# Score products of the first 16 items over 128 contraction rows, 60 of them zero, instead of 68

## The chip, the cores and the metric

One core of one Trainium2 chip runs the whole program in one launch. The metric is device time in microseconds of that core. An execution that is profiled has a span (first to last instruction) and an own time, which is a little longer.

## The reference

Attention with a decaying bias, then a gated two-layer feed-forward, then a soft mixture of experts. The attention is what the change touches:

```python
scores = scale * np.matmul(q, k.transpose(0, 1, 3, 2))        # scale = 1/8, 64 dimensions
cum = np.cumsum(np.maximum(s, 0.0), axis=-1)
bias = -(cum[:, :, :, None] - cum[:, :, None, :])
scores = np.where(causal, -1000000000.0, scores + np.minimum(bias, 0.0))
attn = softmax(scores)
x = attn @ v                       # 4 batches, 8 heads, 576 tokens, 64 dimensions
h = (x @ w1) * (x @ w2) @ w3       # the feed-forward: "gl" products in the kernel
...                                # then 32 slots, 8 experts, and the way back
```

## The kernel before

The attention is cut into items. An item is one head with some of its five query tiles; `ITEMS` lists the first eight heads with tiles 0 to 2 as items 0 to 7, the same heads with tiles 3 and 4 as items 8 to 15, and then the other 24 heads whole, items 16 to 39. For each tile of an item TensorE forms the scores (`att_scores`, L341), VectorE adds the mask and takes the least value (L344), ScalarE takes the exponential (L349), GpSimd divides by the sum (`att_norm`, L362), TensorE turns the tile (`att_transpose`, L377 and L391), ScalarE copies it out (L379, L393), and for each pair of heads TensorE multiplies by the values (`att_pv`, names `x_ps`, recorded under the helper's line L110). A whole block of tokens then goes through the feed-forward (`glu_half`, names `gl`, L439).

The scores of an item contract over 68 rows: 64 dimensions of q and k, and 4 rows that add the decay (`cum` in two parts, and ones). Items 0 to 15 (`n < NF32`) use the float32 tile `raw` itself: rows 0 to 63 come from `qk` (`att_fetch`, L279 to L282), rows 64 to 67 from the decay rows (`att_prep`, L304 for the first two items straight from SBUF, L306 later from the copy `rows_d` in HBM). One float32 product is two records in the profile. Items 16 to 39 split q and k into two parts, `qa` over 128 rows and `qb` over 68 rows, and are not touched.

The `raw` tiles of items 0 to 15 rotate over three tags of two buffers, six buffers in all. A tile framework writes out the order of VectorE, ScalarE, GpSimd and TensorE from its own planning, so an added instruction can move others; SyncE's queue of DMAs keeps the order of the program. Each engine runs its list in that order, and a wait holds up everything behind it on that engine. SyncE also holds up: `v` (L290) has two buffers, so the third load waits until `x_ps` products of the first pair are done, and the loads behind it wait too.

At the start, `decay_rows` computes the decay rows: L148 and L149 (a scan) on VectorE, the casts L159, the differences L160 and negations L162 on VectorE, copies L161 on ScalarE. SyncE then sends them to items 0 and 1 (L304) and to `rows_d` (L166, L167). Beside them the feed-forward's 64-bit weights (`raw_w`, loaded by L178) are converted: L186 on ScalarE, L189, L190, L193 on VectorE, L217 on ScalarE, L218 on GpSimd. Small constants come from the identity (`rep` L771, `half` L776, `part` L939), which GpSimd builds.

Of the kernel before, what the change touches and what calls it, by code (L numbers as in the profile page):

```python
# [10 lines left out]
F32 = mybir.dt.float32  # L11
# [10 lines left out]
P = 128  # L22
B, H, S, D = 4, 8, 576, 64
# [24 lines left out]
def attn_glu_softmoe_kernel(  # L48
# [14 lines left out]
    nc = tc.nc  # L63
# [21 lines left out]
    NRW, SCB, PTB, QAB, VB = 2, 3, 2, 2, 2  # L85
    NF32, NDIR, ND, FAR = 16, 2, 1, 3
# [177 lines left out]
    hd = {}  # L264
    ITEMS = [(h, t) for t in ((0, 1, 2), (3, 4)) for h in range(H)] + [(h, (0, 1, 2, 3, 4)) for h in range(H, NH)]

    def att_fetch(n, ap):
        h, tiles = ITEMS[n]
        if h % 2 == 0:
            b, c = divmod(h // 2, H // 2)  # L270
            for blk, (_, nt, own) in enumerate(BLK):
                if own[0] in tiles:
                    x_t[b, blk, c] = xpl.tile([P, 2, nt], F32R, tag=f"x{blk}", name=f"x_{b}_{blk}_{c}", bufs=NX)
        q0, q1 = QT[tiles[0]][0], sum(QT[tiles[-1]])
        tag = ("raw", "qa", "qb")[n % 3] if n < NF32 else "raw"
        raw = ap.tile([P, 2, S], F32, tag=tag, name=f"raw_{n}", bufs=NRW)
        m = 64 if n < NF32 else P
        if q0:
            nc.sync.dma_start(raw[:m, 0, q0:q1], qk[h, 0, :m, q0:q1])  # L279
            nc.sync.dma_start(raw[:m, 1, :q1], qk[h, 1, :m, :q1])  # L280
        else:
            nc.sync.dma_start(raw[:m, :, :q1], qk[h, :, :m, :q1].rearrange("n p t -> p n t"))  # L282
        hd[n] = dict(raw=raw, q0=q0, q1=q1)
# [9 lines left out]
    def att_prep(n, ap):  # L293
        h, tiles = ITEMS[n]
        t = hd[n]
        raw, q0, q1 = t["raw"], t["q0"], t["q1"]
        if n < NF32:
            rows = raw
        else:
            rows = ap.tile([P, 2, S], F32R, tag="qb", name=f"qb_{n}", bufs=QAB)  # L300
            qa = ap.tile([P, 2, S], F32R, tag="qa", name=f"qa_{n}", bufs=QAB)
        if n < NDIR:
            for a in range(2):
                nc.sync.dma_start(rows[64 + 2 * a : 66 + 2 * a, :, :q1].bitcast(F32), dec[a][h : h + 1, :, :, :q1])  # L304
        else:
            nc.sync.dma_start(rows[64:68, :, :q1].bitcast(F32), rows_d[h].rearrange("a b n t -> (a b) n t")[:, :, :q1])  # L306
        if n < NF32:
            t["mul"] = [rows[:68]]
            return
        rq, rk, qb = raw[:, 0], raw[:, 1], rows  # L310
        nc.vector.tensor_copy(qa[:, 0, q0:q1], rq[:, q0:q1])  # L311
        nc.scalar.dma_start(qb[0:64, 0, q0:q1].bitcast(F32), qa[0:64, 0, q0:q1].bitcast(F32))
        nc.vector.tensor_copy(qa[:, 1, :q1], rk[:, :q1])
        nc.gpsimd.tensor_tensor(  # L314
            out=qb[0:64, 1, :q1], in0=rk[0:64, :q1], in1=qa[0:64, 1, :q1].bitcast(F32), op=ALU.subtract
        )
        nc.gpsimd.tensor_tensor(  # L317
            out=qa[64:, 0, q0:q1], in0=rq[64:, q0:q1], in1=qa[64:, 0, q0:q1].bitcast(F32), op=ALU.subtract
        )
        t["mul"] = [qa, qb[:68]]  # L320
# [317 lines left out]
    def att_steps(ap):  # L638

        groups = [[] for _ in range(B + 1)]  # L640
        N = len(ITEMS)
        for n in range(N + 1):
            tiles = ITEMS[n][1] if n < N else ()
            old = [i for i in ITEMS[n - 1][1] if i] if 0 < n <= N else []
            sc = [(0.2 + 0.3 * i, lambda i=i, n=n: att_scores(n, i, ap)) for i in tiles]
            tr = [(0.2 + 0.3 * i, lambda i=i, n=n: att_transpose(n - 1, i, ap)) for i in old]
            norm = [(0, lambda n=n: att_norm(n - 1))] if 0 < n <= N else []
            prep = [(0, lambda n=n: att_values(n + 1, ap))] if n + 1 < N else []
            d = FAR if n + FAR < NF32 else 1 if NF32 <= n + 1 < N else 0
            if d:  # L650
                prep += [(0, lambda m=n + d: att_prep(m, ap))]
            d = FAR + 1 if n + FAR + 1 < NF32 else 2 if NF32 <= n + 2 < N else 0
            if d:
                prep += [(0, lambda m=n + d: att_fetch(m, ap))]
            blks = [k for k in range(2) if BLK[k][2][0] in ITEMS[n - 1][1]]
            pv = [(1.4, lambda n=n, k=k: att_pv(n - 2, k)) for k in blks] if n > 0 and n % 2 == 0 else []
            groups[min(B, max(0, (n - 1) // H))] += [
                *sc[:1], *norm, *sc[1:2], *prep, *sc[2:3], *tr[:1], *sc[3:4], *tr[1:2], *sc[4:], *tr[2:], *pv
            ]
        return groups  # L660
# [78 lines left out]
    with tc.tile_pool(name="att", bufs=1) as ap:  # L739
        phi_sb = ap.tile([P, KC, NS], F32, name="phi_sb")  # L740
        u_sb = ap.tile([P, FC, NS], F32, name="u_sb")
        decay_fetch()
        fetch_words(0, ap)
        att_fetch(0, ap)
        fetch_words(1, ap)
        att_fetch(1, ap)
        make_identity(nc, ident)
        mask = ap.tile([P, S], F32, name="mask")
# [9 lines left out]
        for n in range(NDIR):  # L758
            att_prep(n, ap)
# [4 lines left out]
        for n in range(NDIR, FAR):  # L764
            att_fetch(n + 1, ap)
            att_prep(n, ap)
# [36 lines left out]
        k = GC - GB  # L803
        steps = steps[GB:]
        run(weave(att[2], weave(steps[:k], prep[CB:]) + steps[k:]))
        for b in range(2, B):
            steps, late = glu_steps(b - 1, late)
            n = len(more) // (B - b)
# [7 lines left out]
    def big(where, name):  # L816
        if where == "w":
            return wp.tile([P, 2048], F32, tag="W", name=name, bufs=NW)
        if where == "t":
            return tp2.tile([P, 2048], F32, name=name)  # L820
        return ep.tile([P, 2048], F32, tag="E", name=name)
# [3 lines left out]
    for i in range(2):  # L825
        t = big("e", f"wo_t{i}").rearrange("p (i c) -> p i c", i=2)
# [3 lines left out]
    for i in range(4):  # L830
        t = big("e", f"w3_t{i}").rearrange("p (i c) -> p i c", i=2)
# [67 lines left out]
    for q in range(4):  # L899
        cols = slice(256 * q, 256 * q + 256)  # L900
        yps = psum(("acc", "sg")[q % 2], f"y_ps_{q}")
        for r in range(2):
            for j in range(4):
                f = 4 * r + j
# [10 lines left out]
    for r in range(2):  # L915
        for c in range(2):
            for j in range(4):
                f = 4 * r + j
# [199 lines left out]
```

## Time and profile before

| what | value |
|---|---|
| median of 3 runs | 566.16 us (562.83 to 568.1) |
| profiled execution, own time | 565.44 us |
| its span | 563.6 us |
| TensorE (PE) busy | 520.0 us, 92% of the span |
| TensorE weight loads (PEld) | 433.9 us, 77% |
| VectorE (DVE) / ScalarE (ACT) / GpSimd (POOL) busy | 316.2 / 310.0 / 196.7 us |
| float32 score records of items 0 to 15 | 96 records, 35.5 us busy |
| mean granted TensorE clock | 0.981 |

The span is the time between first and last instruction of this one execution; its own time is 1.8 us more. A busy TensorE is not TensorE at its peak, since a matmul takes longer at the lower clock and still counts as busy.

### The profile page before, as it was taken

What the parts mean: (1) busy time and instruction counts of PE and PEld (TensorE: products, weight loads), DVE (VectorE), ACT (ScalarE), POOL (GpSimd) and SP (SyncE); (2) the same over time, 40 slices, a digit from 0 to 9 for tenths busy, and PEclk for the clock granted to TensorE, in tenths of its full rate; (3) what the DMA queues carried; (4) which work ended last, traced back from release to release, by engine and by line L of the source; (5) the groups of instructions that cost most, each with busy time, mean ns of one, the idle gap of its engine ahead of it and who ended that gap; (6) DMA issues with size and microseconds to landing.
All of it is one profiled execution on the core that took longest, in us unless ns stands there. A gap on an engine that the chain in (4) does not pass through costs nothing. (4 is left out here: it accounts for less than half of the span.)

```text
span 563.6 us, 11844 instructions
## 1 busy us (share of the span) xinstructions
PE 520.0 (92%) x4288; PEld 433.9 (77%) x4288; DVE 316.2 (56%) x966; ACT 310.0 (55%) x845; POOL 196.7 (35%) x247
## 2 busy tenths in 40 slices
PE   3789899998979999899899999999999999999993
PEld 2566688787768897889889889889988999853452
DVE  7568696889964385736574657446631311243333
ACT  4576586788865675646566567357833321321222
POOL 5475464438745374253354444333210000000000
PEclk9997899999979999999999999999999999999998
DMA  5765966868654173345646563555330999689977
GB/s 157 237 179 178 261 203 215 287 219 261 191 201 119 39 220 109 130 135 179 206 136 213 168 197 104 166 167 172 113 113 1 391 413 381 233 300 421 421 296 244
DMA packets 38809, 118.03 MB, mean 209 GB/s; under 512 B 4224, under 2 KB 10560, under 8 KB 35296
## 3 DMA queue, kind: packets, MB, share of 16 engines
q1 hardware_dynamic: 36832, 113.74, 58.8%
q10 hardware_dynamic: 1920, 3.54, 2.5%
q8 instruction: 34, 0.56, 0.4%
q14 instruction: 23, 0.19, 0.1%
HBM read 102.11 MB, written 11.60 MB: 202 GB/s over the span
## 5 line engine op out<-in xcount | busy, mean ns | idle before, releaser
L439 PE MATMUL gl<-x,w12t 128*128 128x320 f32 (+1 forms) x1536 | 238.3, 304 | 1.3 <-DVE nmax L344 0.7
L439 PEld LDWEIGHTS gl<-x,w12t 128*128 128x128 f32 x1536 | 212.2, 191 | 10.0 <-issue 4.3
L362 POOL TENSOR_SCALAR sc<-sc,rinv 128x64 f32<-128x64 f32 (+4 forms) x160 | 92.4, 594 | 53.9 <-DVE rinv L359 39.2
L349 ACT ACTIVATE sc<-sc,nmax 128x64 f32<-128x64 f32 (+4 forms) x160 | 89.5, 560 | 32.2 <-DVE nmax L344 31.6
L317 POOL TENSOR_TENSOR qa<-raw,qa 64x576 fp32r<-64x576 f32 x24 | 36.5, 1522 | 144.1 <-DVE qa L311 138.3
L344 DVE CUSTOM_DVE_ANT_0 sc<-sc_ps,mask 128x64 f32<-128x64 f32 (+4 forms) x160 | 64.8, 424 | 32.1 <-PE sc_ps L341 29.0
L379 ACT COPY pt<-pt_ps 128x128 f32<-128x128 f32 (+3 forms) x128 | 52.2, 423 | 27.1 <-PE pt_ps L377 16.3
L377 PE MATMUL pt_ps<-ident,sc 128*128 128x128 f32 x320 | 56.8, 288 | 4.9 <-ACT pt L379 2.3
L341 PE MATMUL sc_ps<-qa 128*128 128x64 f32 (+1 forms) x144 | 46.6, 336 | 6.0 <-DVE nmax L344 2.5
L377 PEld LDWEIGHTS pt_ps<-ident,sc 128*128 128x128 f32 x320 | 38.8, 145 | 17.3 <-issue 10.0
L341 PE MATMUL sc_ps<-qb 68*128 68x64 f32 (+1 forms) x144 | 44.2, 310 | 4.2 <-issue 4.2
L110 PE MATMUL x_ps<-pt,v 128*64 128x256 f32 (+1 forms) x384 | 47.5, 353 | 0.0
L445 ACT COPY a<-gl 128x256 f32<-128x256 f32 (+1 forms) x64 | 25.3, 398 | 38.5 <-PE gl L439 34.8
L341 PE MATMUL sc_ps<-raw 68*128 68x288 f32 (+4 forms) x96 | 35.5, 514 | 11.1 <-DMA raw<-rows 9.6
L990 POOL MEMSET ht<- 128x1024 f32 x2 | 1.9, 954 | 107.3 <-DVE ew L894 98.4
L186 ACT ACTIVATE w_w<-raw_w 128x512 f32<-128x512 f32 x32 | 21.6, 676 | 31.6 <-DMA raw_w<-in_w 31.6
L314 POOL TENSOR_TENSOR qb<-raw,qa 64x576 fp32r<-64x576 f32 x24 | 38.2, 1590 | 2.2 <-PE gl L439 0.5
L110 PEld LDWEIGHTS x_ps<-pt,v 128*64 128x64 f32 x384 | 32.0, 138 | 6.7 <-issue 1.0
L341 PEld LDWEIGHTS sc_ps<-qa 128*128 128x128 f32 x144 | 27.7, 192 | 9.1 <-DVE nmax L344 3.5
L427 DVE TENSOR_TENSOR x<-x_ps,x 128x320 fp32r<-128x320 f32 (+1 forms) x32 | 14.0, 455 | 36.2 <-ACT x L426 36.1
L341 PEld LDWEIGHTS sc_ps<-raw 68*128 68x128 f32 x96 | 21.2, 259 | 16.3 <-issue 12.1
L341 PEld LDWEIGHTS sc_ps<-qb 68*128 68x128 f32 x144 | 28.0, 194 | 4.6 <-issue 4.4
(180 smaller groups left out, 785.4 us busy)
## 6 DMA issues: line engine op xcount, KB each, us to landing
ew<-in_ew SPq DMA_DIRECT2D x27, 1024.0 KB
raw_w<-in_w SPq DMA_DIRECT2D x32, 512.0 KB
raw<-in_qk SPq DMA_DIRECT2D x24, 576.0 KB
v<-in_v SPq DMA_DIRECT2D x16, 576.0 KB
raw_w3t<-in_w3t SPq DMA_DIRECT2D x16, 512.0 KB
raw_wot<-in_wot SPq DMA_DIRECT2D x8, 512.0 KB
raw_wo<-in_wo SPq DMA_DIRECT2D x8, 512.0 KB
w_d<-w_w SPq DMA_DIRECT2D x8, 512.0 KB
```

The costliest lines, as they stand in the source:

```text
L110: mm = nc.tensor.matmul(out_, lhs, rhs, start=start, stop=stop)
L186: nc.scalar.activation(out=w, in_=hi.bitcast(F32), func=AF.Copy, scale=F64_SCALE)
L314: nc.gpsimd.tensor_tensor(out=qb[0:64, 1, :q1], in0=rk[0:64, :q1], in1=qa[0:64, 1, :q1].bitcast(F32), op=ALU.subtract)
L317: nc.gpsimd.tensor_tensor(out=qa[64:, 0, q0:q1], in0=rq[64:, q0:q1], in1=qa[64:, 0, q0:q1].bitcast(F32), op=ALU.subtract)
L341: nc.tensor.matmul(pp[:r, : z - a], x[:, 0, q0 : q0 + r], x[:, 1, a:z], start=x is mul[0], stop=x is mul[-1])
L344: nc.vector.tensor_tensor_reduce(out=sc[:r, a:z], in0=pp[:r, : z - a], in1=hd["mask"][:r, m0 : m0 + z - a], scale=-0.125, scalar=3.0e38 if ...
L349: nc.scalar.activation(out=sc[:r, :W], in_=sc[:r, :W], func=AF.Exp, bias=nmax[:r, i : i + 1], scale=-1.0, accum_out=rsum[:r, i, 0:1],)
L362: nc.gpsimd.tensor_scalar(out=sc, in0=sc, scalar1=rinv[:, i : i + 1], scalar2=1.0, op0=ALU.mult, op1=ALU.mult)
L377: nc.tensor.transpose(tp[:, j * P : (j + 1) * P], sc[:, j * P : (j + 1) * P], ident)
L379: t["turned", i] = nc.scalar.copy(out=pt[:, p0 : p0 + step * (i - 1) + 1 : step], in_=tp[:, : i * P].rearrange("p (j q) -> p j q", q=P))
L439: nc.tensor.matmul(acc[:, :nt], w12_t[fc][:, wi, n, kc], x_t[b, blk, kc][:, xi], start=k == 0, stop=k == 3 * KC - 1)
L445: nc.scalar.copy(out=a_sb[:, :nt], in_=acc[:, :nt])
```

## The change

Six tiles of 128 rows take the place of the rotating `raw` tiles, one for each of the six buffers, and are kept. On first use, rows 64 to 127 of each are set to zero, on VectorE for tiles 0, 2 and 4 and on GpSimd for tiles 1, 3 and 5 (64 rows of 2 x 576 values each). DMAs then write rows 0 to 67 as before, and the score products read all 128 rows.

```diff
+    wide = []
+
+    def rows_of(n, ap):
+        k = n % (3 * NRW)
+        if k == len(wide):
+            t = ap.tile([P, 2, S], F32, tag=("raw", "qa", "qb")[k % 3], name=f"wide_{k}", bufs=NRW)
+            (nc.vector, nc.gpsimd)[k % 2].memset(t[64:], 0.0)
+            wide.append(t)
+        return wide[k]
+
     def att_fetch(n, ap):
...
-        tag = ("raw", "qa", "qb")[n % 3] if n < NF32 else "raw"
-        raw = ap.tile([P, 2, S], F32, tag=tag, name=f"raw_{n}", bufs=NRW)
+        if n < NF32:
+            raw = rows_of(n, ap)
+        else:
+            raw = ap.tile([P, 2, S], F32, tag="raw", name=f"raw_{n}", bufs=NRW)
         m = 64 if n < NF32 else P
...
         if n < NF32:
-            t["mul"] = [rows[:68]]
+            t["mul"] = [rows]
             return
```

Lines behind the new function stand 12 further down after the change (L341 becomes L353, L189 stays). The change moves instructions on four engines, all in about the first fifth of TensorE's list; SyncE's order stays.

On VectorE, from its first instruction up to the scan, before:

```order
L117 MEMSET warm 128x1
L148 TENSOR_SCALAR dec<-dec 32x576
L771 TENSOR_REDUCE rep<-ident 128x32
L776 TENSOR_REDUCE half<-ident 128x1
L939 TENSOR_REDUCE part<-ident 128x1
L149 SCALAR_TENSOR_TENSOR dec<-dec 32x576
```

and after:

```order
L117 MEMSET warm 128x1
L273 MEMSET wide_112 64x1152
L273 MEMSET wide_158 64x1152
L273 MEMSET wide_184 64x1152
L148 TENSOR_SCALAR dec<-dec 32x576
L189 TENSOR_SCALAR w_w_0_0_207<-w_w_0_0_207 128x512
L149 SCALAR_TENSOR_TENSOR dec<-dec 32x576
```

Three zero fills come first, and the first weight step L189, which waits for ScalarE's L186, now stands ahead of the scan L149.

On VectorE again, from the last cast of the decay rows to the first negation L162, on which SyncE's second L304 waits, before:

```order
L159 CAST rows_132<-dec 32x64
L942 TENSOR_SCALAR part<-part 128x2
L160 TENSOR_TENSOR rows_131<-dec,rows_130 32x320
L160 TENSOR_TENSOR rows_131<-dec,rows_130 32x192
L189 TENSOR_SCALAR w_w_0_0_202<-w_w_0_0_202 128x512
L160 TENSOR_TENSOR rows_132<-dec,rows_132 32x64
L162 TENSOR_SCALAR rows_131<-rows_131 32x320
```

and after:

```order
L159 CAST rows_134<-dec 32x64
L189 TENSOR_SCALAR w_w_0_1_263<-w_w_0_1_263 128x512
L193 SCALAR_TENSOR_TENSOR w_w_0_0_207<-raw_w_0_0_109,w_w_0_0_207 128x512
L160 TENSOR_TENSOR rows_133<-dec,rows_132 32x320
L160 TENSOR_TENSOR rows_133<-dec,rows_132 32x192
L160 TENSOR_TENSOR rows_134<-dec,rows_134 32x64
L190 SCALAR_TENSOR_TENSOR w_w_0_1_263<-raw_w_0_1_115,w_w_0_1_263 128x512
L783 TENSOR_REDUCE rep<-ident 128x32
L788 TENSOR_REDUCE half<-ident 128x1
L951 TENSOR_REDUCE part<-ident 128x1 x2
L162 TENSOR_SCALAR rows_133<-rows_133 32x320
```

The weight steps L189 of the second half (it waits for ScalarE's second L186), L193 and L190, and the constants, now stand ahead of L162. On ScalarE the second L186 likewise moves ahead of the three copies L161.

On TensorE, item 5's scores and the beginning of the first pair's `x_ps` products, before:

```order
L341 MATMUL sc_ps_0_0_404<-raw_212 128x64
L341 MATMUL sc_ps_1_0_414<-raw_212 128x192
L341 MATMUL sc_ps_2_0_422<-raw_212 128x320
L341 MATMUL sc_ps_0_0_452<-raw_252 128x64
L110 MATMUL x_ps_0_281<-ptd_219,v_176 64x64
L110 MATMUL x_ps_0_281<-ptd_268,v_176 64x64
```

and after:

```order
L353 MATMUL sc_ps_0_0_407<-wide_217 128x64
L403 MATMUL ptd_ps_281<-ident,sc_171 128x128 x3
L353 MATMUL sc_ps_1_0_417<-wide_217 128x192
L110 MATMUL x_ps_0_286<-ptd_225,v_180 64x64
L353 MATMUL sc_ps_2_0_424<-wide_217 128x320
L353 MATMUL sc_ps_0_0_454<-wide_112 128x64
L353 MATMUL sc_ps_1_0_464<-wide_112 128x192
L110 MATMUL x_ps_0_286<-ptd_273,v_180 64x64
```

The bulk of the pair's products now follows one score product of item 6 later; otherwise the order of this stretch is much the same.

## Rows read from the trace of the kernel before

**Rows 1.** By stretch: us; busy PE, PEld, DVE, ACT, POOL; granted clock; DMA share.

```profile
19.10:29.70 10.60, 10.57 (x33) 8.53 (x33) 6.22 (x28) 6.52 (x24) 6.01 (x9) 1.00 0.89 269
29.70:33.10 3.40, 3.40 (x25) 3.20 (x25) 3.24 (x14) 3.03 (x13) 3.40 (x6) 1.00 0.00 1
40.00:43.40 3.40, 2.23 (x11) 1.44 (x10) 3.06 (x7) 2.01 (x6) 0.59 (x2) 1.00 0.87 264
43.40:47.50 4.10, 4.10 (x10) 2.61 (x11) 3.20 (x8) 2.14 (x8) 1.33 (x1) 0.50 0.85 271
47.50:50.20 2.70, 2.70 (x12) 2.11 (x10) 2.22 (x9) 2.16 (x6) 0.93 (x2) 0.50 0.12 42
60.50:63.90 3.40, 1.48 (x9) 0.82 (x7) 2.31 (x5) 3.07 (x8) 0.00 (x0) 1.00 0.97 280
63.90:67.30 3.40, 3.23 (x11) 2.68 (x12) 3.37 (x8) 2.29 (x7) 1.28 (x1) 0.50 0.97 224
...
234.50:237.90 3.40, 2.12 (x17) 1.93 (x15) 3.40 (x5) 2.17 (x8) 2.04 (x2) 1.00 0.12 27
```

**Rows 2.** TensorE's groups by shape from 19.6 to 29.7 us.

```profile
L341 PE MATMUL sc_ps<-raw 68*128 68x320 f32 x8 | 5.1, 741 | 0.0
...
L377 PE MATMUL pt_ps<-ident,sc 128*128 128x128 f32 x4 | 1.3, 424 | 0.0
```

**Rows 3.** TensorE's groups by shape from 68 to 100 us.

```profile
L341 PE MATMUL sc_ps<-raw 68*128 68x288 f32 x20 | 6.2, 406 | 0.0
L377 PE MATMUL pt_ps<-ident,sc 128*128 128x128 f32 x30 | 4.5, 276 | 0.0
```

**Rows 4.** TensorE's groups by shape from 29.7 to 33.1 us, the values' products.

```profile
L110 PE MATMUL x_ps<-pt,v 128*64 128x256 f32 x4 | 1.3, 647 | 0.0
```

**Rows 5.** What SyncE's queue waited for from 19 to 52 us.

```profile
SPq L290 <- PE pt_ps L377: 9.3, 2, 6.7
SPq L290 <- PE x_ps L110: 6.1, 1, 6.1
```

**Rows 6.** TensorE's groups by shape, whole span: 128-row and 68-row products of equal width.

```profile
L341 PE MATMUL sc_ps<-qa 128*128 128x288 f32 x48 | 15.0, 321 | 1.4 <-DVE nmax L344 1.4
L341 PE MATMUL sc_ps<-qb 68*128 68x288 f32 x48 | 14.0, 299 | 0.0
```

**Rows 7.** Timeline of the first 14 us: start, duration, engine, line.

```profile
0.98 0.58 POOL L749 MEMSET mask<- 128x576 f32 x1
...
2.78 0.86 DVE L148 TENSOR_SCALAR dec<-dec 32x576 f32<-32x576 f32 x1 [1.92 <-DMA dec<-in_s]
...
4.09 1.33 DVE L149 TENSOR_TENSOR_SCAN dec<-dec 32x576 f32<-32x576 f32 x1
4.77 0.67 ACT L186 ACTIVATE w_w<-raw_w 128x512 f32<-128x512 f32 x1 [2.55 <-DMA raw_w<-in_w]
...
7.32 0.48 DVE L162 TENSOR_SCALAR rows<-rows 32x320 f32<-32x320 f32 x2
...
7.99 0.69 ACT L186 ACTIVATE w_w<-raw_w 128x512 f32<-128x512 f32 x1 [1.18 <-DMA raw_w<-in_w]
...
9.05 0.69 DVE L193 SCALAR_TENSOR_TENSOR w_w<-raw_w,w_w 128x512 uint32<-128x512 uint32 x1
...
9.61 4.61 PE L341 MATMUL sc_ps<-raw 68*128 68x64 f32 x12 [9.61 <-DMA raw<-rows]
```

**Rows 8.** VectorE's groups by line in the first 13 us.

```profile
L190 DVE SCALAR_TENSOR_TENSOR w_w<-raw_w,w_w 128x512 int32<-128x512 int32 x2 | 1.4, 679 | 0.0
...
L160 DVE TENSOR_TENSOR rows<-dec,rows 32x320 fp32r<-32x320 f32 (+2 forms) x3 | 0.9, 340 | 0.0
...
L189 DVE TENSOR_SCALAR w_w<-w_w 128x512 int32<-128x512 int32 x2 | 0.8, 417 | 0.2 <-ACT w_w L186 0.2
...
L939 DVE TENSOR_REDUCE part<-ident 128x1 f32<-128x64 f32 x2 | 0.4, 189 | 0.0
L771 DVE TENSOR_REDUCE rep<-ident 128x32 f32<-128x128 f32 x1 | 0.3, 350 | 0.0
```

## The prediction

> **What bounds the kernel now.** I read the stretches of the first 67 us first, then TensorE's groups by shape in two of them, then SyncE's waits, then the start. TensorE is what the kernel waits for nearly everywhere (92% busy), so what counts is where it is slow and where it is idle. In the first 67 us it is both. From 19.1 to 29.7 us it is busy for 10.57 of 10.60 us [rows 1], yet the same turning product that takes 276 ns later takes 424 ns here [rows 2, 3]: it runs at the lower of its two clock levels, 1.2 instead of 2.4 GHz. The column of the granted clock says 1.00 there and is not to be believed before its first entry: the durations say half. It still says so at 29.7 to 33.1 us, where the values' products take 647 ns [rows 4]; after 33.1 us products are short. From 43.4 to 50.2 us the column itself says 0.50, again with TensorE busy all the time (4.10 of 4.10 and 2.70 of 2.70 us), and once more from 63.9 to 67.3 us [rows 1]. In the first two of these stretches TensorE holds up the loads too: SyncE waits 6.1 us for the `x_ps` products and up to 6.7 us for a turning product before it may send the next `v`, and the weights queued behind `v` wait as long [rows 5].
>
> So a busy TensorE alone does not raise the clock. What the slow stretches have in common is float32 score products over 68 rows: from 19.6 to 29.7 us the widest of them alone are 5.1 us of TensorE's time, against 1.3 us of one kind of turning product [rows 2]. The clock rose after the 128-row `x_ps` products from 29.7 us on, and again after 128-row `gl` products in 47.5 to 50.2 us. It fell at 43.4 us after a stretch in which TensorE was busy 2.23 of 3.40 us, mostly with 68-row scores, and at 63.9 us after one with 1.48 of 3.40 us; but from 234.5 us, busy 2.12 of 3.40 us and mostly with `gl`, it kept its clock [rows 1]. My reading: 68 rows count for less than 128. It is only a reading, since those scores differ from `gl` in being float32 too.
>
> The Trainium skill, TensorE: Matmul & The Clock Gate, Part 1: The HAM clock gate, says that sustained matmul activity releases the throttle and speaks of how busy TensorE has been, not of rows. By that alone the stretch from 19.1 us, full of matmuls, should have been fast soon after its start; the trace disagrees (424 against 276 ns). If rows do not matter, as that section reads, the change buys no clock at all, which is the first rival below.
>
> **The change part by part.** The products themselves: 96 records now read 128 rows. The nearest rows are 128-row and 68-row products of equal width, 321 and 299 ns [rows 6], the first of which starts each tile and waits. A cost of 22 ns each would be 96 x 0.022 = 2.1 us; I take 0, because a product is paid by its columns: TensorE was already full at 19.1 us with products that follow each other without idle time. The zero rows add nothing to any DMA.
>
> The zero fills: the nearest row is GpSimd's fill of 576 columns in 0.58 us [rows 7], so 1.16 us for 1152 columns, three on VectorE and three on GpSimd, 3.5 us each. If they begin at about 1 us, as GpSimd's fill does, VectorE is done at 4.5 us at worst and with L148 (0.86 us) at 5.4 us; at best they take half of that. Either way the next in its list, L189, waits until ScalarE's first L186 ends at 4.77 + 0.67 = 5.44 us [rows 7]. So the fills themselves cost nothing; if they ran into that cover they would cost what exceeds 5.4 us. GpSimd's two later fills stand before the identity, which by the same row's rate is then ready at about 9 us (an estimate), before VectorE asks for it after 11 us.
>
> The moved instructions cost more. The scan L149 stands behind L189 and starts at about 5.44 + 0.42 = 5.9 us instead of 4.09. Behind the casts, VectorE now waits for the second L186, which ends at 7.99 + 0.69 = 8.68 us because its weights land then [rows 7]. Before the two L162 are done come L189 0.42, L193 0.69, three L160 0.9, L190 0.68, `rep` 0.35 and three small reductions of 0.19, then the L162 pair itself 0.48 [rows 7, 8]: 4.1 us, less some 0.06 us at each of ten steps, since neighbours overlap (three L160 of 0.340 us are 0.9 us busy, not 1.02): 3.5 us, done at 12.2 us. Before it was 7.32 + 0.48 = 7.80 us, and the first product came 1.81 us after, at 9.61 us, on the landing of the last decay rows [rows 7]. Now that is 14.0 us: **4.4 us late**. Without the overlap it is 5.0 us; if the constants hid somewhere, 3.6 us. Nothing soaks it up at once: SyncE is stuck at its second L304 until L162, with q and k of item 2, the next weights and the decay rows' copy behind it, so items 2 and on shift as a whole, and so does ScalarE, whose next L186 waits for those weights.
>
> The clock, first stretch. If 128 rows raise it, the run of products that began at 19.1 us begins at 23.5 us, and the clock rises some time after. In the trace it rose 3.4 us after `x_ps` had set in (29.7 to 33.1) and 2.6 us after `gl` had (47.5 to 50.2) [rows 1]; I allow 5 us for a start at a bad moment. Of 14.0 us at half clock 9.0 are left, of which a TensorE bound by nothing else would save half, 4.5 us. But ScalarE is busy 6.52 of 10.60 and 3.03 of 3.40 us in it, VectorE 3.24 and GpSimd 3.40 of the last 3.40 [rows 1], and weights come no earlier until SyncE is freed. I take 60%, **2.7 us**, with 0 and 4.5 as ends. It passes on, because the end of `x_ps` frees SyncE [rows 5]; the products stand in almost the same place of TensorE's list as before. The products between 14.0 and 18.6 us may raise the clock as well, but the items behind them still wait for their DMAs.
>
> The clock, second stretch: 6.8 us of full TensorE at half clock, with SyncE waiting for its turning product [rows 1, 5]. At full clock 3.4 us less; VectorE (3.20 of 4.10 us) and the loads take some back: **2.8 us**, between 0 and 3.4. What is late next are the weights around 60 us, which come at DMA share 0.97 while TensorE has 1.48 us of work in 3.40 [rows 1]; they are sent by the same queue, hence earlier too. That idle time, not the rows, lowers the clock at 63.9 us, so I leave the third stretch as it is; if it went, 3.23 / 2 = 1.6 us more.
>
> Sum: +4.4 - 2.7 - 2.8 = **-1.1 us** on the profiled execution's own 565.44 us, 564.3. That execution lies 0.7 us under the median of 566.16, on which the forecast is given: **565 us**. Later stages keep their order and TensorE is busy 92% of the span, so a shift of everything reaches the end as it is.
>
> **The rivals.** First, slower: rows do not count, the half-clock stretches stay, and the late start is all there is. For it: the products in these stretches are float32, and it may be that which keeps the clock low; no stretch of float32 products over 128 rows alone is there to tell the two apart. Against: the rise at 33.1 us came on `x_ps` products, which are float32 as well, though two of them run side by side. Price +4.4 us (3.6 to 5.0), and up to 2.1 us more if a wider product costs: 566.2 + 4.4 = 570.6, up to 573. It decides if products at 23.5 to 37 us keep the long durations (741 ns for 320 columns). Second, faster: the clock rises in the first burst already or soon after 23.5 us, other engines yield more than I grant, and the fall at 63.9 us goes too, with the late start near its lower end: +4.0 - 4.5 - 3.4 - 1.6 = -5.5, 560.7 us. For it: SyncE's long waits end on TensorE [rows 5]; against: ScalarE and VectorE near their limit at 30 us. Third, that the late start is hidden: items 2 on would have to wait for something other than SyncE's queue; then the gains stand alone, 566.2 - 5.5 = 560.7 as well. I find no such thing in the rows.
>
> **How the numbers follow.** About 1% (5.7 us) is what a measurement of this kernel can tell from no change. Chances: the forecast (rows count, late start about paid back, 562 to 568) 0.55; first rival 0.28; second 0.12; third 0.05. The range leaves out the upper tail of the first rival and the far end of the gains: 560 to 572 us. Faster by over 1% (below 560.5) needs all of the second or third and some luck: 0.14. Slower by over 1% (above 571.8) is the first rival with its worse prices: 0.16. Within 1%: 0.70.
>
> **What would show it.** The first score product at 13.5 to 14.7 us; VectorE's fills done before 5.4 us; turning products of 276 ns well before 33 us after allowing for the shift, and products of 288 columns at about 406 ns [rows 3] around 45 us; SyncE's waits before `v` shorter by some 3 us each. I am wrong if the start is not late, if the clock stays at half with 128 rows, or if it rises and the stretch is no shorter, which would mean that ScalarE, VectorE or the loads set its pace.

## The result and the profile after

The changed kernel takes 571.15 us (median of 20 runs), the kernel before 565.83 us in the same comparison (20 runs): a ratio of 1.0093, 95% interval 1.0069 to 1.0117, so 5.3 us slower. The forecast was 1.1 us faster. The profiled execution of the changed kernel has a span of 569.4 us; all rows in this section are from it. Lines are 12 further down than before (L341 is L353, L290 is L302).

The start first: the timeline of VectorE in the first 14 us, and TensorE's first product (start, duration, engine, line).

```profile
3.57 1.02 DVE L273 MEMSET wide<- 64x1152 f32 x1 [0.19 <-issue]
4.62 0.85 DVE L148 TENSOR_SCALAR dec<-dec 32x576 f32<-32x576 f32 x1
5.87 1.29 DVE L189 TENSOR_SCALAR w_w<-w_w 128x512 int32<-128x512 int32 x1 [0.40 <-ACT w_w L186]
7.08 1.33 DVE L149 TENSOR_TENSOR_SCAN dec<-dec 32x576 f32<-32x576 f32 x1
...
8.99 0.67 DVE L159 CAST rows<-dec 32x320 fp32r<-32x320 f32 x3
9.59 0.41 DVE L189 TENSOR_SCALAR w_w<-w_w 128x512 int32<-128x512 int32 x1
...
12.59 0.99 DVE L162 TENSOR_SCALAR rows<-rows 32x320 f32<-32x320 f32 x3
```

```profile
15.29 1.09 PE L353 MATMUL sc_ps<-wide 128*128 128x64 f32 x3 [15.29 <-DMA wide<-rows]
```

GpSimd's two later fills, in the timeline of GpSimd:

```profile
5.82 2.33 POOL L273 MEMSET wide<- 64x1152 f32 x2
```

The reader is to see three things against [rows 7]: the last of VectorE's fills ends at 4.59 us, and L148 stands right behind it, 1.84 us late; the scan L149 starts at 7.08 instead of 4.09 us; the first product comes at 15.29 instead of 9.61 us, 5.7 us late where 4.4 was foretold.

Then the stretches (us; busy time of PE, PEld, DVE, ACT, POOL with counts; granted clock; DMA share; GB/s), which answer to [rows 1]:

```profile
24.00:27.46 3.46, 2.59 (x9) 2.14 (x9) 0.60 (x4) 1.48 (x6) 2.45 (x4) 1.00 0.79 247
27.46:30.87 3.41, 3.41 (x13) 2.93 (x13) 2.04 (x11) 1.73 (x7) 0.00 (x0) 1.00 0.94 273
30.87:34.29 3.42, 2.67 (x16) 1.74 (x14) 3.03 (x16) 3.02 (x13) 1.76 (x3) 1.00 0.96 295
34.29:37.70 3.41, 2.91 (x27) 2.11 (x27) 2.37 (x12) 3.41 (x13) 2.41 (x5) 1.00 0.23 52
37.70:41.11 3.41, 1.54 (x10) 1.35 (x10) 1.98 (x11) 2.54 (x10) 3.41 (x6) 1.00 0.76 241
41.11:44.53 3.42, 1.70 (x5) 0.83 (x3) 2.57 (x7) 1.45 (x6) 2.58 (x4) 0.50 0.87 269
44.53:47.94 3.41, 3.41 (x11) 2.17 (x10) 1.37 (x4) 2.07 (x5) 3.11 (x6) 0.50 0.02 7
...
61.30:64.50 3.20, 0.80 (x7) 0.49 (x5) 3.05 (x6) 1.00 (x4) 1.92 (x2) 1.00 0.93 273
65.00:68.42 3.42, 3.42 (x24) 3.22 (x24) 1.61 (x3) 1.91 (x6) 0.47 (x1) 0.50 1.04 257
```

As before, the column says 1.00 up to its first entry, here at 30.87 us, and is not to be believed until then. The clock rises at 30.87 us, before any values product has run (the first starts at 32.4 us, their bulk at 35.0): score products and turning products did it alone. But TensorE then runs dry, that is, it has less work than time: 1.54 of 3.41 us busy from 37.7 us on, and the clock falls at 41.11 us for 6.8 us. What TensorE waited for from 36 to 50 us (total, number of waits, longest):

```profile
PE sc_ps L353 <- DMA wide<-rows_d: 4.1, 2, 2.4
```

These are two waits for decay rows; the kernel before has no wait for decay rows there. In the view of SyncE's waits from 19 to 52 us [rows 5], one line stands for two waits:

```profile
SPq L302 <- PE pt_ps L389: 13.6, 2, 8.7
```

The queue stands 8.7 us before the fourth `v`, and the decay rows that TensorE waits for are queued behind the third (sent at 36.60 and 39.13 us). The `v` loads go out at these times (timeline of SyncE's queue):

```profile
36.21 0.33 SPq L302 DMA_DIRECT2D v<-in_v  x1
49.65 0.33 SPq L302 DMA_DIRECT2D v<-in_v  x1
57.52 0.33 SPq L302 DMA_DIRECT2D v<-in_v  x1
```

Before, they went out at 32.28, 39.58 and 51.52 us: 3.9, 10.1 and 6.0 us late. In TensorE's list the changed kernel has item 8's three score products (of 448, 288 and 288 columns) ahead of the second pair's `x_ps`. TensorE's timeline from 36 to 50 us, with item 7's and item 8's scores and the bulk of `x_ps`:

```profile
39.57 1.33 PE L353 MATMUL sc_ps<-wide 128*128 128x64 f32 x6 [2.37 <-DMA wide<-rows_d]
43.13 3.75 PE L353 MATMUL sc_ps<-wide 128*128 128x448 f32 x6 [1.72 <-DMA wide<-rows_d]
...
48.58 0.71 PE L110 MATMUL x_ps<-pt,v 128*64 128x256 f32 x6
```

and in the kernel before, where `x_ps` stands first:

```profile
38.50 0.71 PE L110 MATMUL x_ps<-pt,v 128*64 128x256 f32 x6
...
39.75 1.89 PE L341 MATMUL sc_ps<-raw 68*128 68x448 f32 x6
```

Equal products of the two kernels, matched one to one and sorted by their time in the kernel before, stand 4.4 us later at 32 to 36 us, 10.1 at 36 to 40 us, 5.1 at 65 to 80 us, 3.8 at 160 to 235 us, 5.7 at the end. This lag is used below for other runs too.

### The profile page after: what moved, and what is told of

Same layout as the page of the kernel before. It is cut to its first block, busy times and chain, and to the rows that moved or that the text cites. A ratio compares the mean times of both kernels' runs of the same rounds, so it can differ in the third digit from the quotient of the medians.

```text
span 569.4 us, 11854 instructions
## 1 busy us (share of the span) xinstructions
PE 519.6 (91%) x4288; PEld 433.9 (76%) x4288; DVE 317.6 (56%) x969; ACT 310.7 (55%) x845; POOL 201.5 (35%) x250
## 5 line engine op out<-in xcount | busy, mean ns | idle before, releaser
L361 ACT ACTIVATE sc<-sc,nmax 128x64 f32<-128x64 f32 (+4 forms) x160 | 89.6, 561 | 37.7 <-DVE nmax L356 37.1
L329 POOL TENSOR_TENSOR qa<-raw,qa 64x576 fp32r<-64x576 f32 x24 | 36.6, 1524 | 144.7 <-DVE qa L323 131.8
L391 ACT COPY pt<-pt_ps 128x128 f32<-128x128 f32 (+3 forms) x128 | 52.2, 423 | 26.1 <-PE pt_ps L389 15.3
L353 PE MATMUL sc_ps<-wide 128*128 128x288 f32 (+4 forms) x96 | 34.2, 489 | 21.1 <-DMA wide<-rows 15.3
L353 PE MATMUL sc_ps<-qa 128*128 128x64 f32 (+1 forms) x144 | 47.1, 339 | 6.2 <-DVE gC L469 2.6
L389 PEld LDWEIGHTS pt_ps<-ident,sc 128*128 128x128 f32 x320 | 39.5, 147 | 16.0 <-issue 9.4
L457 ACT COPY a<-gl 128x256 f32<-128x256 f32 (+1 forms) x64 | 25.4, 399 | 38.8 <-PE gl L451 35.1
L353 PE MATMUL sc_ps<-qb 68*128 68x64 f32 (+1 forms) x144 | 44.5, 312 | 2.1 <-issue 2.1
L353 PEld LDWEIGHTS sc_ps<-wide 128*128 128x128 f32 x96 | 19.6, 243 | 27.1 <-DVE part L954 15.3
L186 ACT ACTIVATE w_w<-raw_w 128x512 f32<-128x512 f32 x32 | 21.6, 674 | 29.4 <-DMA raw_w<-in_w 29.3
L353 PEld LDWEIGHTS sc_ps<-qa 128*128 128x128 f32 x144 | 27.9, 194 | 9.3 <-DVE nmax L356 3.6
L439 DVE TENSOR_TENSOR x<-x_ps,x 128x320 fp32r<-128x320 f32 (+1 forms) x32 | 14.0, 455 | 35.2 <-ACT x L438 35.1
L361 ACT ACTIVATION_READ_ACCUMULATOR sc<-sc,nmax 128x1 f32 x160 | 30.6, 191 | 0.0
```

Source lines behind the costliest of these rows:

```text
L186: nc.scalar.activation(out=w, in_=hi.bitcast(F32), func=AF.Copy, scale=F64_SCALE)
L329: nc.gpsimd.tensor_tensor(out=qa[64:, 0, q0:q1], in0=rq[64:, q0:q1], in1=qa[64:, 0, q0:q1].bitcast(F32), op=ALU.subtract)
L353: nc.tensor.matmul(pp[:r, : z - a], x[:, 0, q0 : q0 + r], x[:, 1, a:z], start=x is mul[0], stop=x is mul[-1])
L361: nc.scalar.activation(out=sc[:r, :W], in_=sc[:r, :W], func=AF.Exp, bias=nmax[:r, i : i + 1], scale=-1.0, accum_out=rsum[:r, i, 0:1],)
L389: nc.tensor.transpose(tp[:, j * P : (j + 1) * P], sc[:, j * P : (j + 1) * P], ident)
L391: t["turned", i] = nc.scalar.copy(out=pt[:, p0 : p0 + step * (i - 1) + 1 : step], in_=tp[:, : i * P].rearrange("p (j q) -> p j q", q=P))
```

## The experiments

**How they are made.** The planner answers every edit with another order, which is an edit of its own. Runs 1 to 4 leave it free. From run 5 on every instruction of TensorE, VectorE, ScalarE and GpSimd has its place from a written table, taken from the kernel before ("old order") or from the changed one ("new order"); SyncE's order is the same in all. The table adds dependencies that only order an engine's own list, and no wait:

```python
for a, b in zip(seq, seq[1:]):           # seq: one engine's instructions in the order wanted
    tc.add_manual_dep(b, a.name, order, reason="order")     # order: DependencyClass.NoSync
```

First rise is the first entry of the granted clock; turning products get short there in every run. Ratios are to the kernel before on the same chip, with the 95% interval.

| run | rows | fills | order | first product | first rise | third v | ratio |
|---|---|---|---|---|---|---|---|
| before | 68 | none | old | 9.6 us | 33.1 us | 32.3 us | 1 |
| changed | 128 | at start | new | 15.3 | 30.9 | 36.2 | 1.0093 (1.0069 to 1.0117) |
| 1 | 68 | at start | planner's | 15.1 | 65.3 | 39.0 | 1.0222 (1.0171 to 1.0273) |
| 2 | 128 | at start | planner's | 14.7 | 18.6 | 35.1 | 1.0081 (1.0039 to 1.0122) |
| 3 | 128 | at start | planner's | 11.6 | 27.0 | 34.9 | 1.0068 (1.0040 to 1.0097) |
| 4 | 128, items 0, 1: 68 | later | planner's | 12.1 | 26.4 | 30.9 | 1.0202 (1.0150 to 1.0255) |
| 5 | 128 | at start | old | 13.2 | 17.9 | 36.6 | 1.0044 (1.0008 to 1.0079) |
| 6 | 68 | none | new | 14.8 | 39.5 | 38.6 | 1.0181 (1.0120 to 1.0242) |
| 7 | 68 | at start | new | 14.9 | 40.3 | 38.5 | 1.0245 (1.0187 to 1.0302) |
| 8 | 68 | at start | old | 13.2 | 48.3 | 38.0 | 1.0085 (1.0050 to 1.0119) |
| 9 | 128 | at start | PE new, rest old | 12.3 | 16.0 | 36.4 | 1.0126 (1.0086 to 1.0167) |
| 10 | 128 | at start | PE old, rest new | 15.2 | 20.1 | 35.6 | 1.0144 (1.0098 to 1.0189) |
| 11 | 128 | hidden | old | 9.6 | 14.2 | 34.0 | 0.9980 (0.9950 to 1.0011) |
| 12 | 68 | hidden | old | 9.6 | 44.1 | 33.6 | 1.0033 (0.9999 to 1.0068) |
| 13 | 128 | hidden | old, own buffer for third v | 9.6 | 14.5 | 26.4 | 0.9964 (0.9933 to 0.9996) |
| 14 | 68 | hidden | old, own buffer for third v | 9.6 | 41.8 | 25.9 | 0.9971 (0.9942 to 1.0001) |

### Runs 1 to 4: one part undone, planner free

Run 1:

```diff
-            t["mul"] = [rows]
+            t["mul"] = [rows[:68]]
```

> The changed kernel with its fills, its kept buffers and its order at the start, but the score products contract over 68 rows again. Theory (rows count): the first product is at 15.3 us as in the changed kernel, the 320-column score products keep 741 ns until values products have run, and the clock rises only behind these, at 37 to 42 us instead of 30.9; the 1.8 us that the changed kernel had won back by then are lost again: 573 us (571.5 to 576). Rival (the rise at 30.9 us came from the later start or the moved order, rows do not matter): a rise near 31 us and 571.2 us within 1.

576.81 us. No rise at 31 us and none at 40: TensorE stays at half clock until 65.3 us, and turning products take 439 ns from 45 to 64 us. The theory (rows count) holds, at a higher price than it gave, but the planner's order differs from the changed kernel's as well; run 7 takes that away.

Run 2 (`pv_last[2]` is the second pair's last values product):

```diff
+                if n == 8 and i == tiles[0]:
+                    tc.add_manual_dep(mm.ins, pv_last[2].ins.name, order, reason="order")
```

> The changed kernel, with one dependency more: item 8's first score product stands behind the values products of the second pair, as in the kernel before. The start stays late (first product 15.3 us). Theory (the moved place of item 8's scores makes SyncE wait 8.7 us for a turning product and loses the second stretch): no SyncE wait there over 6 us, the fourth v is sent at 43 to 46 us instead of 49.65, no half-clock stretch at 41 to 48 us or a shorter one, and the kernel takes 566 to 568.5 us. Rival (the stretch was lost to late rows and the late start alone, the place does not matter): 571 us within 1, half clock at 41 to 48 us as before.

570.02 us. SyncE's longest wait is 6.5 us, the fourth `v` goes out at 46.7 us, yet half-clock stretches stay (39.1 to 42.5, 45.9 to 49.4 us) and the ratio is that of the changed kernel. The planner also moved many other rows of TensorE's list, so this neither clears nor convicts the place of item 8's scores; run 9 asks again.

Run 3 (`decay_end`: the last copy L161 on ScalarE and the last L162 on VectorE):

```diff
+        if k == 1:
+            behind_decay(cast, 0)          # ScalarE's second L186 behind L161
...
+            if k < 2:
+                behind_decay(shift, 1)     # VectorE's L189 of both halves behind L162
```

> The changed kernel, fills and 128 rows as they are, with VectorE's and ScalarE's conversion of the first weights held behind the decay rows by order alone. Theory (of the 5.7 us of late start 1.85 us are the fills themselves, since L148 starts at 4.62 instead of 2.78 us, and the rest are instructions that moved ahead of the decay rows): first product at 11 to 12 us; if the shift passes on whole, 571.2 - 3.8 = 567.4 us (565.5 to 569). Rival of the prediction (fills cost nothing): first product at 9.6 to 10 us, 565.5 us. Rival (the start is soaked up by loads later): 570 to 571.5 us.

568.23 us. The first product comes 1.96 us late instead of 5.7: the theory's 1.85 us is met, the prediction's zero is not. The time lies in the theory's range too.

Run 4:

```diff
-            (nc.vector, nc.gpsimd)[k % 2].memset(t[64:], 0.0)
+        if NDIR <= n < NDIR + 3 * NRW:
+            nc.gpsimd.memset(wide[k][64:], 0.0)
...
-            t["mul"] = [rows]
+            t["mul"] = [rows[:68] if n < NDIR else rows]
```

> No fills at the start: items 0 and 1 contract over 68 rows, GpSimd fills the rows of items 2 to 7 behind the decay rows, all later items as in the changed kernel over 128 rows. VectorE's and ScalarE's order at the start is that of the kernel before; item 8's scores still stand ahead of the second pair's values. Theory: first product at 9.6 us, clock up at 24 to 30 us, before values products could raise it, and 571.2 - 5.7 = 565.5 us with the loss of the moved order still in it (562.5 to 567). Rival (rows do not matter): clock up near 33 us, 566 to 569 us. Rival (the fills are paid wherever they stand, GpSimd's six of 1.05 us holding up rows and weights): 569 us or more, GpSimd or DMA ahead of TensorE's idle time at 14 to 25 us.

577.15 us, and the first product at 12.1 us instead of 9.6, which none of the three foretold. The lag is 1.7 us at 60 us and 11.3 us at 230 us; the planner's new list differs from both others there, and which difference costs it stays open. Inconclusive on the fills, and the reason for the written tables.

### Runs 5 to 8: fills, rows and order one by one

Run 5 is the changed kernel with the old order; run 8 the same with `rows[:68]`. Run 7 is the changed kernel with its own order and `rows[:68]`. Run 6 is run 7 without the `memset`.

> The fills and the 128 rows of the changed kernel, but on TensorE, VectorE, ScalarE and GpSimd every instruction stands where it stood in the kernel before (a written-out order that adds no wait); the fills stand first on VectorE, one first and two behind the decay rows on GpSimd. Theory (128 rows raise the clock; the loss is in the moved instructions): first product near 11.5 us, 1.9 late as in the third run; full clock before 30 us; no half clock at 43 to 50 us or a short one; 1.9 - 2.7 - 2.8 on the kernel before, 562 us, ratio 0.994 (0.988 to 1.000). Rival (the gain is not to be had even so, since items wait for their decay rows and weights): ratio 1.003 to 1.008 as in the third run.

> The kernel before with its 68 rows and no fills, but with every instruction of TensorE, VectorE, ScalarE and GpSimd where it stands in the changed kernel (written-out order, no wait added). Theory (the order costs by itself): first product at 12.5 to 13.5 us, item 8's scores ahead of the second pair's values, SyncE's wait before the fourth v 8 us or more; ratio 1.010 to 1.018 (570 to 575 us), since no rows win anything back. Rival (the order costs only through the fills that caused it): ratio 1.000 to 1.005.

> The changed kernel in all, its fills and its exact order (written out), with 68 rows in the products instead of 128: the rows alone. Theory (rows count): half clock kept until behind the values products, some 38 us or later, instead of 30.9; slower than the changed kernel by 2 to 6 us, 573 to 577 us, ratio to the kernel before 1.013 to 1.022. Rival (rows do not matter): ratio 1.009 as the changed kernel, full clock at 31 us.

> The fills alone: 68 rows, every other instruction where it stood in the kernel before. Theory (the fills cost the start 1.9 us and nothing else): first product near 11.5 us, clock as in the kernel before but 2 us later, ratio 1.003 (1.001 to 1.006). The difference to the run with 128 rows and the same order is what rows are worth: 5 us by the prediction's two terms; by the rival (rows worth nothing) both runs take the same time.

Runs 5, 6, 7 and 8 take 568.07, 576.90, 579.69 and 570.08 us.

**Rows count.** Run 7 differs from the changed kernel in the rows alone (and in that its order is written out) and is 1.5% (8.6 us) slower, more than the 2 to 6 us expected; the two intervals are far apart. TensorE's groups by shape from 24 to 34 us, run 7:

```profile
L391 PE MATMUL sc_ps<-wide 68*128 68x320 f32 x7 | 4.7, 764 | 0.0
```

and the changed kernel, with the rise in the middle of it:

```profile
L353 PE MATMUL sc_ps<-wide 128*128 128x320 f32 x8 | 4.1, 600 | 0.0
```

In the table every kernel with 128 rows has its first rise at 14 to 31 us, and every one with 68 at 33 to 65 us; four pairs differ in the rows alone (run 7 and the changed kernel, 8 and 5, 12 and 11, 14 and 13). That a written order by itself costs little is seen in run 12, 0.3% above the kernel before. The first rival of the prediction (rows don't count) is refuted as to the clock.

**The order costs by itself, and more than its late start.** Run 6 has no fills and 68 rows, as the kernel before, and loses 1.81% (10.2 us). Its first product is 5.2 us late (12.5 to 13.5 us was expected, it came at 14.8); at 65 to 80 us the lag is 12.6 us. SyncE's waits from 9 to 66 us:

```profile
SPq L338 <- PE pt_ps L425: 16.5, 2, 9.9
SPq L338 <- PE x_ps L146: 7.5, 1, 7.5
```

Before, the longest of these was 6.7 us [rows 5]. The late start does not pass through as a shift: from 32 to 36 us to 36 to 40 us the lag grows from 6.4 to 13.2 us here and from 4.4 to 10.1 us in the changed kernel, both in the new order. In the old order it goes from 4.5 to 4.5 us with 128 rows (run 5) and from 5.8 to 7.6 us with 68 (run 8). So most of the growth belongs to the order, and it falls where the second pair's `x_ps` stand.

**The fills alone cost 4.8 us** (run 8; ratio 1.0085, where 1.003 was expected). Their late start, 3.6 us, is more than the 1.96 of run 3, because in these two runs the casts L159 (here L196) meet GpSimd's two later fills. Timelines of VectorE and of GpSimd in run 5:

```profile
7.32 2.46 DVE L196 CAST rows<-dec 32x320 fp32r<-32x320 f32 x3
```

```profile
7.29 2.27 POOL L311 MEMSET wide<- 64x1152 f32 x2
```

The three casts took 0.67 us in the changed kernel, where no fill ran beside them.

**Run 5 misses its expectation** (562 us) by 6 us: 3.6 us of start instead of 1.9, then 4.2 us won back by 65 to 80 us (a lag of -0.6 us there), somewhat less than foretold; but 2.5 us are lost behind 220 us, where the clock falls from 239.8 to 243.2 and from 280.8 to 284.2 us. The profile of the kernel before has no falls there, the changed kernel's has (242.5 and 283.5 us), but kernels with 68 rows have them too (run 8 at 280.4 us, run 12 at 238.6, run 14 at 236.4 and 277.3). Between runs 5 and 8 the rows are worth 0.4% (2.3 us), not 5; the two intervals overlap.

### Runs 9 and 10: which half of the new order

One engine's table is exchanged for the other kernel's: TensorE's alone is new in run 9, TensorE's alone old in run 10.

> The fifth run (fills, 128 rows, old order on all engines) with TensorE's list alone as in the changed kernel. The changed kernel stands 0.49% (2.8 us) above the fifth run. Theory (item 8's scores ahead of the second pair's values cost the second stretch): first product as in the fifth run, 13.2 us; the fourth v is sent at 47 us or later instead of 44.1; ratio 1.008 to 1.012. Rival (the 2.8 us are the later start of the moved instructions on VectorE and ScalarE): ratio 1.004.

> The changed kernel with TensorE's list alone as in the kernel before; the moved instructions of VectorE, ScalarE and GpSimd stay. First product 15.3 us. Theory (TensorE's list costs the 2.8 us): fourth v at 46 to 47 us, ratio 1.003 to 1.006. Rival (the start costs it): ratio 1.008 to 1.010, since 5.7 - 3.6 = 2.1 us of later start remain.

571.14 and 572.51 us. Each half costs against run 5, 0.8% and 1.0% with intervals apart. Run 9 does as its theory had it: TensorE's list alone puts item 8's scores at 43.9 us, ahead of the second pair's `x_ps`, after waits for decay rows, and the fourth `v` goes out at 48.1 instead of 44.1 us. That the place of these scores delays the fourth `v` is therefore shown with the other lists old; how much of the 0.8% is theirs, and not that of the other rows moved in TensorE's list, is not. Both expectations miss run 10. There TensorE has its old list and waits for ScalarE's copies, whose list is the new one (TensorE's waits from 36 to 50 us in run 10, then the only such wait in run 5):

```profile
PE ptd_ps L441 <- ACT pt L429: 2.7, 1, 2.7
PE pt_ps L427 <- ACT pt L429: 2.4, 1, 2.4
```

```profile
PE pt_ps L427 <- ACT pt L429: 0.7, 1, 0.7
```

So each engine's list suits the other lists of its own kernel. Both halves together (the changed kernel) stand 0.5% above run 5, but the intervals overlap with run 5's and with those of runs 9 and 10: that two halves cost less than one is not shown, and the 2.8 us cannot be shared out between start and TensorE's list.

### Runs 11 and 12: fills in idle time

```diff
+            low = t[64:, :, :320]
+            if k < 2:
+                fills.append((nc.vector.memset(low, 0.0), 1))
+            else:
+                zero = hd["mask"][64:, :320].unsqueeze(1).broadcast_to([64, 2, 320])
+                fills.append((nc.scalar.copy(out=low, in_=zero), 1 if k < 5 else 5))
+            fills.append((nc.gpsimd.memset(t[64:, :, 320:], 0.0), 19 if k < 3 else 23))
```

The number beside each fill is its place in its engine's list. Run 12 is the same with `rows[:68]`.

> 128 rows, every other instruction where it stood in the kernel before, and the fills cut to the columns that the first eight items read and laid into idle time: two on VectorE before the decay sums land, four on ScalarE (copies of zero columns of the mask), the other columns on GpSimd from 15 us on. Theory: first product at 9.6 to 10.2 us, full clock by 28 us, 4.2 us won between the start and 65 us as between the two runs with fills and the old order; ratio 0.990 to 0.996 (561 to 564 us). Rival (clock falls later than 65 us take it back, as near 240 and 281 us in the fifth run): 0.997 to 1.002 although 65 us is passed 4 us early.

> The same as the run before it in all, with 68 rows in the products: what the hidden fills still cost. Theory (they lie in idle time): ratio 1.000 (0.998 to 1.003), first product at 9.6 to 10.2 us, full clock near 33 us. Rival (fills cost wherever they stand): 1.004 or more. The difference to the run before it is what the rows are worth at an unchanged start: 3 to 5.5 us by the theory, 0 if rows do not count.

564.43 and 565.42 us, beside 564.98 for the kernel before. The start is untouched (9.6 us in both), so fills need not cost anything there. But the ratio of run 11 is its rival's, not its theory's, and rows are worth 0.53% (3.0 us) between the two, with overlapping intervals, not 5.5, although the clock is up as early as 14.2 us. By 65 to 80 us run 11 is 2.4 us early and run 12, with 68 rows and first at full clock at 44.1 us, 2.2. Run 12 was to equal the kernel before, so a gap of 2 us between two single profiles shows nothing. Windows of run 11 show where the faster TensorE does not help:

```profile
21.02:24.43 3.41, 3.41 (x12) 2.59 (x11) 1.18 (x8) 1.23 (x4) 2.06 (x4) 0.50 0.97 271
24.43:27.84 3.41, 2.33 (x16) 1.79 (x15) 2.81 (x12) 2.88 (x11) 1.80 (x4) 1.00 0.99 238
27.84:31.25 3.41, 1.36 (x7) 0.67 (x6) 1.61 (x6) 1.68 (x6) 2.15 (x4) 1.00 0.77 178
31.25:34.67 3.42, 2.86 (x21) 2.75 (x22) 3.33 (x15) 3.20 (x12) 2.00 (x4) 0.50 0.00 0
34.67:38.08 3.41, 3.41 (x12) 2.47 (x12) 2.13 (x10) 2.52 (x11) 3.41 (x5) 0.50 0.64 182
```

and the same first two stretches of run 12, at half clock:

```profile
24.43:27.84 3.41, 3.41 (x13) 2.56 (x12) 2.76 (x11) 3.02 (x12) 1.47 (x3) 1.00 1.10 256
27.84:31.25 3.41, 2.95 (x11) 2.20 (x10) 2.10 (x6) 2.30 (x11) 2.49 (x5) 1.00 0.53 146
```

(Run 12's column is again the false 1.00 ahead of its first entry.) At full clock TensorE has 2.33 and 1.36 us of work in 3.41 and waits for GpSimd (1.1 us) and for decay rows (1.3 us); then the clock falls, and the values' products, on which the third `v` waits, run at half. The third `v` goes out at 34.0 us with 128 rows and at 33.6 with 68: nothing is gained up to there.

### Runs 13 and 14: a buffer of its own for the third v

```diff
+            if n == 5:
+                vt = gu.tile([P, 640], F32, tag="gU", name="v_5", bufs=2).rearrange("p (k e d) -> p k e d", k=5, e=2)
+            else:
+                vt = ap.tile([P, 9, 2, D], F32, tag="v", name=f"v_{n}", bufs=VB)
```

> The eleventh run (128 rows, hidden fills, old order) with the third v load in a buffer of its own, one that the feed-forward part does not use yet, so that SyncE need not wait for the first pair's values products; order on all engines unchanged. Theory (the loop between v and the values products takes half of what rows are worth): SyncE sends the third v at 26 us instead of 34.0, no half clock from 31 to 38 us, ratio 0.985 to 0.993. Rival (the loads are the bound at a DMA share of 0.99, the wait for v only hides it): ratio 0.998 within 0.003, as the eleventh run.

> The same with 68 rows. By the theory the buffer alone gains less at half clock, since TensorE then has work all the time: ratio 0.994 to 1.001, and 128 rows are worth 5 us or more between the two runs, against 3 us between the eleventh and twelfth. By the rival the two runs stand 3 us apart as those two, or the buffer gains as much here as with 128 rows.

563.79 and 563.87 us, beside 565.31 for the kernel before. The queue is freed (timeline of SyncE's queue in run 11, then in run 13, the third load):

```profile
34.02 0.33 SPq L345 DMA_DIRECT2D v<-in_v  x1
```

```profile
26.38 0.43 SPq L348 DMA_DIRECT2D v<-in_v  x1
```

but the theory is wrong: with 128 rows the buffer gains 0.16% (inside the intervals), with 68 rows 0.62%, and the rows are now worth 0.07% (0.4 us, far inside the intervals). At 65 to 80 us equal products are 4.7 us early in run 13 and 5.1 in run 14. In run 13 the stretches around the rise read:

```profile
24.20:27.60 3.40, 2.53 (x14) 1.79 (x13) 2.76 (x11) 3.02 (x11) 1.40 (x3) 0.92 0.99 282
27.60:31.00 3.40, 1.82 (x13) 1.11 (x11) 2.25 (x9) 2.51 (x11) 2.73 (x5) 1.00 1.02 303
```

and in run 14, at half clock (its column is the false 1.00):

```profile
24.20:27.60 3.40, 3.40 (x12) 2.70 (x12) 2.80 (x12) 2.87 (x11) 1.80 (x4) 1.00 1.01 289
27.60:31.00 3.40, 3.40 (x16) 2.89 (x17) 2.84 (x11) 2.90 (x10) 2.85 (x4) 1.00 1.01 307
```

TensorE is dry at full clock here too, with the DMA share at 0.99 and 1.02, ScalarE busy 3.02 of 3.40 us and no wait for `v`. Its two waits in these stretches are 0.9 us for GpSimd's division and 1.5 us for ScalarE's copy of a turned tile. ScalarE's timeline of run 13 shows what stands before that copy:

```profile
28.74 0.67 ACT L222 ACTIVATE w_w<-raw_w 128x512 f32<-128x512 f32 x1 [0.89 <-DMA raw_w<-in_w]
...
30.63 0.30 ACT L451 COPY ptd<-ptd_ps 128x192 f32<-128x192 f32 x1
```

ScalarE waits for weights to land, converts them (L222), works through the exponentials behind them without a gap, and only then copies. So in this trace the loads reach TensorE by way of ScalarE's list, near to what the rival had; no run takes that wait away. Run 13 is the fastest kernel of this study, 0.36% under the kernel before, but not by its 128 rows: run 14 has nearly the same without them.

## Why the prediction was wrong, point by point

- **That 128 rows raise the clock: right.** Run 7 and the table of first rises show it, and it is the rows alone.
- **The start, 4.4 us late (3.6 to 5.0): too small, 5.7.** The moved instructions alone are 5.2 us (run 6), the fills 0.2 to 0.5 on top of them (run 7, the changed kernel). In the sum, the second L189 was to start at 8.68 us and did so at 9.59 us (the second L186 ended at 9.52; in run 6, without fills, at 9.04), and the first L162 took 0.72 us instead of 0.31, beside GpSimd's L218. So the second L162 ended at 13.5 instead of 12.2 us (13.0 in run 6); the first product followed it by the 1.8 us foretold. "The fills themselves cost nothing" holds for the start, nearly, only behind the moved instructions: alone, they make it 1.96 us late (run 3) or 3.6 us (runs 5 and 8).
- **The step that failed: the late start and the moved list were priced as a plain shift of 4.4 us**, with "the products stand in almost the same place of TensorE's list as before". The list was compared up to item 6 only; item 8's scores ahead of the second pair's values came after that. Without rows and fills, the new order costs 10.2 us (run 6), 5.0 more than its own late start, and the lag jumps where these values' products stand. Set against the forecast's sum, +4.4 for start and order, 0 for the fills and -5.5 for the rows, the runs give +10.2 (run 6), +3.6 (run 7 less run 6; the intervals overlap) and -8.6 (run 7 against the changed kernel): 5.2 us, where 5.3 were measured. The order is off by 5.8 us; the errors of the other two terms nearly cancel. Run 9 shows TensorE's list as one part of it (0.8% with the other lists old); how the rest falls on the other moved rows stays open (runs 2 and 10).
- **First stretch -2.7, second -2.8: no order gave this 5.5.** In the changed kernel's own order rows are worth 8.6 us (run 7). A likely reason, not tested by itself, is that this order makes more of the kernel wait for a TensorE at half clock. In the old order, the one that the prediction reckoned with, they are worth 2.3 us (runs 5 and 8) and 3.0 us (runs 11 and 12), both with overlapping intervals, and with the third `v` in its own buffer nothing measurable. The misreading was to take a TensorE that is full at half clock for what the kernel waits for: at full clock nearly the same stretch has it busy 2.33 and 1.36 of 3.41 us (run 11). The prediction's last paragraph had named this outcome as a sign of being wrong: the clock "rises and the stretch is no shorter".
- **The second stretch did not go, it came back**: half clock from 41.1 to 47.9 us, after TensorE had been busy 1.54 of 3.41 us. The prediction had seen that idle time lowers the clock (for the third stretch, which stayed as foretold, 65.0 to 68.4 us), and did not ask whether a faster TensorE makes such idle time. The Trainium skill, TensorE: Matmul & The Clock Gate, section HAM oscillation — how this bites in real kernels, describes just this loop: compute shorter than the wait for the next data, the clock falls in the wait, and the next block starts slow. Run 11's five rows above agree, though of TensorE's 2.4 us of waits there only 1.3 are for data from a DMA and 1.1 are for GpSimd.
- **The first rival came nearest in number (570.6) and is wrong in mechanism**: the clock did rise. That 571.15 us lies inside the forecast's 560 to 572 us is luck too: the forecast's parts are off in both directions.
- **Falls near 240 and 282 us** were in no one's account. Behind 235 us the changed kernel loses 1.9 us (3.8 to 5.7 us late) and run 5 2.5 us. The 128 rows are not needed for them, since runs 8, 12 and 14 have such falls with 68. Each kernel has one profile, and the mean granted clock of the kernel before alone goes from 0.965 to 0.993 over its executions, so whether the change makes them likelier is not settled.

## What to carry to other kernels

Before pricing a faster engine, take the stretch at the faster rate and add up what the others need in it: an engine that is full at half clock may be dry at full clock, and then the clock falls again. Where a planner sets the order, an edit is two edits; compare the whole list of the engines that wait, and time the order alone. The price of a part depends on the rest: here rows were worth 8.6 us in one order and 3.0 us or less in another, and fills 4.8 us or nothing measurable, by what else stood in the way.

## What the runs showed of the hardware

- The rows of the contraction count for the clock, zeros too: 60 zero rows move the first rise from 40.3 to 30.9 us at equal order (run 7 and the changed kernel), and from 48.3 to 17.9, 44.1 to 14.2 and 41.8 to 14.5 us in three more pairs (runs 8 and 5, 12 and 11, 14 and 13).
- VectorE and GpSimd hold each other up in some instructions: three casts take 2.46 us beside GpSimd's fills and 0.67 without, and L189 1.29 beside one and 0.41 without; the scan L149 takes 1.33 us either way. The Trainium skill, SBUF — State Buffer, section SBUF: two separate sides, says that a GpSimd operation and some VectorE operations take a shared port in turns, and that the loser waits for the whole instruction; these rows agree. In run 11, where ScalarE's copies did four of the early fills and GpSimd's came after 15 us, the first product stayed at 9.6 us.
- A fill of 64 x 1152 float32 takes VectorE 1.02 us, and three of them in a row start 1.20 us apart (1.16, 2.37 and 3.57 us in the changed kernel); GpSimd's first takes 1.05 us.
